# A fused packed-attention and feed-forward kernel: a new order of steps for the start, batch 0 in 256 and 320 tokens, batch 1's first shares turned by TensorE, and one remainder's products ahead of the packs

## The chip, the cores and the metric

One core of a Trainium2 chip runs the whole program. The metric is the device time of one execution in microseconds; a figure for a kernel is the median of several runs. The engines are TensorE (PE: products, and transposes with an identity), VectorE (DVE), ScalarE (ACT), GpSimd (POOL) and SyncE (SP), whose queue issues nearly all transfers. Each works off its own list in order and waits on semaphores for the others.

## The reference

```
p_packed = softmax(p k^T / 8) v             8 batches, 8 heads, 576 tokens, 32 packs, 64 dimensions
out      = softmax(q p_packed^T / 8) p_packed
x        = out, heads side by side          (4608 tokens, 512)
h        = x w_in                           (512 x 2048)
y        = (h * sigmoid(h)) w_out           (2048 x 512)
```

All in float32; the weights `w_in` and `w_out` come to the device as the bits of float64 numbers, and the kernel makes float32 numbers of them itself.

## The kernel before, in words

`p_packed` is never multiplied by the second shares. For each batch the kernel multiplies the 32 packs of each head into `w_in` (the class `Packs`: "pack products", 64-row tiles, line 232 through `heads`), which gives a small matrix per batch; the hidden layer is then the second shares times that matrix. Products of full size are taken in three terms of a rounded upper part (`hi`) and the remainder (`lo`): the upper part is rounded by ScalarE (`upper`, `g_values`), the lower is a subtraction on VectorE (`lower`, line 225, 464, 493, 551).

The work is cut into units of one batch and 128 of the 2048 hidden columns. A unit has `h` (`h_products`, line 525: 12 products, 288 tokens wide), `g` (`h_values`, lines 543 to 546: the activation of `h` on ScalarE), `l` (`h_lower`, line 551) and `o` (`out_products`, line 561: 12 products, 512 wide). The first four units of batch 0 (`u < WHOLE`) are taken in plain float32, each in two halves of the tokens (`h0.0` and `h0.1`). Of each half's 288 tokens 256 go through `o` in the unit; the 32 left over are kept in `rest`, for two batches together, and make four "rest" units, each of 12 products. `out_rows` (lines 588 to 612) takes the sums out of PSUM.

Per batch the attention goes through steps that the code names by a letter: `aS1.0` is `scores2` of batch 1, half 0. First attention: `as` scores, `ac` copy, `am` maximum, `ax` exponential (line 278), `at` turning of the shares (`turned1`, lines 285 to 297), `ay` (`spread1`, lines 299 to 316), `aa` packed products (line 330), `an` normalising (340), `ai` and `aj` the turned packs (349, 353). Second attention: `aS` scores, `aT` blockwise transposes on VectorE, `aM` maximum and subtraction (`less2`), `aX` exponential, `aD` sum, reciprocal and multiplication (`shares2`), `aH` and `aL` upper and lower part. Batch 0 alone holds its scores by tokens (`ON_TOKENS`): `aC` copies them (374), `aB` turns them on TensorE (382), and `aU` turns the shares back (402, 404), `aF` copies them out (449).

For batch 0, `turned1` transposes on TensorE. For the others VectorE transposes blocks of 32 (line 291) and `spread1` moves the blocks with 16 transfers issued by SP (line 309).

The weights come in 20 chunks, the first eight of 512 columns a partition, the others of 1024. `FIRST` and `CHUNKS` take `w_in` and `w_out` in turn. A chunk passes `wf` (fetch, line 186), `ws` (two operations of ScalarE, 192 and 193), `wz` (bound and sign, 197 and 198, on VectorE), `wj` (shift on VectorE, 204, and addition, 205: VectorE for `w_in`, POOL for `w_out`), and for `w_out` `wu` and `wl` (221, 225). `PLACES` says where the raw bits wait: in one of two staging buffers, or in the part of `win` that is filled later; a fetch into a place that is still in use waits on SP, with all that stands behind it in SP's list.

The order of all this up to the 32nd unit is written in the string `ORDER`, whose steps are put into the engines' lists as they stand. `W6` is six products with the identity that keep TensorE busy (line 139). PSUM has two double buffers for sums (`sum_banks`, two pairs) and two for everything else (`two_banks`: pack products, scores, hidden products). After `ORDER` a loop runs over the remaining units, the four rest units of batches 0 and 1 first, where `packs_in(2, 1, 2)` makes two pack products for batch 2.

Of the kernel before, what the change touches and what calls it, by code (L numbers as in the profile page):

```python
# [11 lines left out]
I32 = mybir.dt.int32  # L12
# [22 lines left out]
REST = HS - MAIN  # L35

# [17 lines left out]
W6 k0 as0.0 W1 as0.1 am0.0 wf0 wf1 am0.1 ax0.0 ax0.1 ar0 v0 ws0 wz0 W4 at0.0 ay0.0 at0.1 ay0.1 wf2 ws1 ws2 wj0 W7  # L54
aa0 an0 W1 ai0 wz2 aj0 q0 W1 pp0 aS0.0 aC0.0 pu0 W1 aS0.1 aB0.0 aC0.1 wj2 pp1 wz1 wj1 wf3 ws3 aM0.0 aX0.0 wf4 ws4
aB0.1 aM0.1 aX0.1 aD0.0 W15 aU0.0 wf5 ws5 wf6 ws6 aD0.1 wz4 aF0.0 W2 h0.0 pu1 k1 g0.0 wz6 aU0.1 aF0.1 wj6 as1.0
ac1.0 wu1 h1.0 g1.0 wf7 wf8 aH0.1 wz5 h0.1 g0.1 h1.1 ws7 v1 wz3 as1.1 wj3 ac1.1 wj5 wj4 g1.1 am1 o0.0 ax1.0 ax1.1
pp3 wz7 wj7 wf9 pp2 pu2 o1.0 at1.0 at1.1 pu3 o0.1 h2.0 h2.1 ws8 g2.0 g2.1 ws9 aL0.1 wz8 o1.1 h3.0 h3.1 wf10 ws10 wj8
# [5 lines left out]
l14 h15 ws16 o13 g15 l15 ax2.0 h16 wz16 wl15 ax2.1 h17 o14 o15 wf17 wj16 g16 l16 wf18 h18 g17 e15.1 l17 e15.0 h19
ws17 o16 wz17 wj17 g18 l18 ws18 o17 pp8 wf19 o18 at2.0 at2.1 ay2 g19 l19 pu8 ws19 pl8 h20 g20 h21 o19 wz18 h22 wj18
wu18 ar2 l20 wz19 wj19 g21 h23 wl18 o20 l21 o21 wu19 wl19 g22 l22 aa2 g23 l23 an2 pp9 pu9 pl9 pp10 o22 pu10 pl10 h24
h25 o23 b0 e23.0 g24 h26 l24 e23.1 o24 g25 ai2 l25 o25 g26 l26 aj2 aS2.1 aT2.1 aM2.1 aX2.1 aS2.0 aT2.0 o26 h27 h28
g27 l27 aM2.0 g28 l28 h29 o27 aD2.1 g29 aX2.0 h30 aH2.1 h31 l29 aD2.0 o28 o29 g30 l30 g31 l31 aH2.0 aL2.0 aL2.1 o30
o31 g32 b1 l32 v3 e31.0 pp11 pu11 e31.1 pl11 k3
# [4 lines left out]

ON_TOKENS = (0,)
# [8 lines left out]
def packed_attention_ffn(ctx: ExitStack, tc: tile.TileContext, pkT, qT, v, w_in, w_out, out):  # L84
# [26 lines left out]
    ident = const.tile([P, P + 352], F32, name="ident")  # L111
# [55 lines left out]
    class Weights:  # L167
# [22 lines left out]
        def scale(self, n):  # L190
            low, up = self.raw[n]
            nc.scalar.activation(low, low.bitcast(U32), AF.Copy, scale=2.0**-29)  # L192
            nc.scalar.activation(up.bitcast(F32), up.bitcast(F32), AF.Copy, scale=2.0**-112)  # L193

        def sign(self, n):
            low, up = self.raw[n]
            nc.vector.tensor_scalar(up.bitcast(F32), up.bitcast(F32), TOP, -TOP, op0=ALU.min, op1=ALU.max)  # L197
            nc.vector.scalar_tensor_tensor(low, up, -(2**31), low, op0=ALU.bitwise_and, op1=ALU.bitwise_or)  # L198

        def join(self, n):  # L200
            f, nf, inner = CHUNKS[n]
            low, up = self.raw[n]
            z = win[:, f : f + nf].rearrange("p f i n -> p (f i n)") if inner else self.whole(n).bitcast(I32)
            nc.vector.tensor_scalar(z, up, 3, None, op0=ALU.logical_shift_left)  # L204
            (nc.vector if inner else nc.gpsimd).tensor_tensor(z, z, low, ALU.add)  # L205
# [20 lines left out]

    def heads(bank, lhs, rhs):

        for par in range(2):
            r = slice(D * par, D * par + D)  # L230
            for i in range(NI):
                nc.tensor.matmul(bank(par)[NP * i : NP * i + NP], lhs(r, i), rhs(r, i), start=True, stop=True)  # L232
# [4 lines left out]
    class Attention:  # L237
# [3 lines left out]
        def __init__(self, b):  # L241
            self.b, self.half, self.turns, self.back, self.shares = b, {}, {}, {}, {}
# [42 lines left out]
        def turned1(self, par):  # L285
            if self.b:

                if par == 0:
                    self.turn = scratch(S)
                blocks = self.turn.rearrange("p (t r x) -> p t r x", r=2, x=NP)  # L290
                nc.vector.transpose(blocks[:, :, par], self.e1[:, par].rearrange("p (t x) -> p t x", x=NP))
                return
            ps = self.turns[par] = sum_banks()
            for c in range(5):
                n = min(P, S - c * P)
                bank = ps[:n, 1, :P] if c == 4 else ps[:n, 0, c * P : c * P + P]
                nc.tensor.transpose(bank, self.e1[:, par, c * P : c * P + n], ident)

        def spread1(self, par=None):
            if not par:  # L300
                self.e1T = scratch(5 * P)
            if self.b:

                self.e1T = self.e1T.rearrange("p (c i rx) -> p c i rx", c=5, i=NI)
                for i in range(NI):
                    for at in range(P // NP):
                        some = self.turn[NP * i : NP * i + NP].rearrange("p (t rx) -> p t rx", rx=2 * NP)
                        some = some[:, at :: P // NP]
                        nc.sync.dma_start(self.e1T[NP * at : NP * at + NP, : some.shape[1], i], some)
# [59 lines left out]
        def copied2(self, hf):  # L369
# [3 lines left out]
            at = slice(0, HS + REST) if hf == 0 else slice(HS + REST, S)  # L373
            nc.scalar.copy(self.s2[:, :, at], self.half[hf][:, :, : at.stop - at.start])

        def spread2(self, hf):
# [3 lines left out]
            for par in range(2):  # L380
                for c, s in enumerate((HS + REST, HS + REST + P) if hf else (0, P, HS + REST - P)):
                    nc.tensor.transpose(ps[:, par, P * c : P * c + P], self.s2[:, par, s : s + P], ident)
# [12 lines left out]
        def back2(self, hf):  # L395

            ps = self.back[hf] = two_banks() if self.b else sum_banks()
            left = slice(P - REST * (2 - hf), P - REST * (1 - hf))
            for par in range(2):
# [3 lines left out]
                some = self.half[0][1][left, par, MAIN:]  # L403
                nc.tensor.transpose(ps[:, par, MAIN:HS], some, ident[left, left])

        def less2(self, hf):
            if self.b in ON_TOKENS:
# [4 lines left out]
                nc.vector.tensor_tensor(t, ps, each, ALU.subtract)  # L412
# [5 lines left out]
            nc.vector.tensor_tensor(s2v, s2v, each, ALU.subtract)  # L418
# [9 lines left out]
        def shares2(self, hf):  # L428
            if self.b in ON_TOKENS:
# [5 lines left out]
                nc.vector.tensor_tensor(t, t, each, ALU.mult)  # L435
                return
            s2, e2 = self.half[hf]
# [6 lines left out]
            nc.vector.tensor_tensor(e2v, e2v, each, ALU.mult)  # L444
            nc.vector.transpose(s2, e2)

        def whole2(self, hf):
            a2 = made["whole", hf] = self.shares[hf] = a2p.tile([P, 2, HS], F32, name="a2_lo")
            nc.scalar.copy(a2, self.back[hf][:, :, :HS])

        def upper2(self, hf):
            hi = a2p.tile([P, 2, HS], F32R, name="a2_hi")
            lo = a2p.tile([P, 2, HS], F32R, name="a2_lo")
# [57 lines left out]
    def h_products(u, hf=None):  # L511
# [4 lines left out]
        for h in range(2)[half_or_all(hf)]:  # L516
# [6 lines left out]
            for n, (p, a, par) in enumerate(todo):  # L523
                bank = ps[:, h if hf is None else 0, :HS]
                nc.tensor.matmul(bank, p[:, par, cols], a[:, par], start=(n == 0), stop=(n == len(todo) - 1))  # L525

    def h_values(u, hf=None):
# [12 lines left out]
        ps, to = made.pop(("h", u, hf)), rest[:, f, b % 2]  # L540
# [5 lines left out]
        nc.scalar.activation(to, ps[..., MAIN:HS], AF.Silu)  # L546
# [41 lines left out]
    def out_rows(u, h):  # L588
# [3 lines left out]
        if more:  # L592
            o = osb.tile([P, 2, DM], F32, name="o")
            half = DM // 2
            nc.scalar.copy(o[:, 0, :half], sums[:, 0, :half])
            nc.vector.tensor_copy(o[:, 0, half:], sums[:, 0, half:])
# [17 lines left out]
    def load_parts(b):  # L614
# [18 lines left out]
        "wz": weights.sign,  # L633
# [11 lines left out]
    names |= dict(n="scaled1", i="turned", j="packs", S="scores2", T="turned2", M="less2", X="exps2", D="shares2")  # L645
# [101 lines left out]
def _laid_out(q, k, v, p, moe_w_in, moe_w_out):  # L747
# [40 lines left out]
```

## Time and profile before

| | us |
|---|---|
| median of 3 runs (lowest, highest) | 710.49 (709.82, 710.53) |
| the profiled execution | 710.59 |
| its span | 708.8 |
| TensorE busy | 696.7 |
| VectorE busy | 332.4 |
| ScalarE busy | 328.5 |
| POOL busy | 21.0 |

The span runs from the first to the last instruction that the profiler recorded; the execution's own time is 1.8 us more. A busy TensorE means that some product was under way; since products overlap and their ends are modelled, their durations add up to more than that. In the rows of instructions the first number is the start, the second the duration, then come engine, line, operation, what is written and read, its shape, the count where several were merged, and in brackets the idle time before it with what ended that. In the rows of stretches the columns are the stretch, its length, the busy time of PE, PEld (weight load), DVE, ACT and POOL, the clock granted to TensorE as a share of full speed, the share of the DMA engines, and GB/s.

### The profile page before, as it was taken

To read this page: it belongs to the slowest core of one execution; us is meant where nothing else is said; L and a number is where in the kernel's file an instruction comes from. 1 tells how busy PE (TensorE), PEld (TensorE's weight loads), DVE (VectorE), ACT (ScalarE), POOL (GpSimd) and SP (SyncE) were. 2 spreads that over 40 slices of the span, in tenths; PEclk is the share of its full clock that TensorE was granted. 3 is DMA by queue.
4 is the path that set the end of the run, shared out by engine and by line. 5 is a ranking of instruction groups with operands and counts; after the bars stand their busy time and mean duration, and the time that the engine had idled before them with its cause. 6 is when DMAs were issued, how large, how long until landed. Compare 5 with 4: busy or idle time off the path is not lost.

```text
span 708.8 us, 12103 instructions
## 1 busy us (share of the span) xinstructions
PE 696.7 (98%) x5060; PEld 564.7 (80%) x5060; DVE 332.4 (47%) x491; ACT 328.5 (46%) x614; POOL 21.0 (3%) x16
## 2 busy tenths in 40 slices
PE   8999999999999999999999999999999999999997
PEld 6647779877868888888888888878878788888886
DVE  4989985944642346332552315433362333622112
ACT  4896858634534325362542625453353533533221
POOL 0202020100000000000000000000000000000000
PEclk9999999999999999999999999999999999999999
DMA  9755653315032140302212022121301210010002
GB/s 356 304 205 198 222 218 149 125 60 193 0 130 82 34 147 1 127 21 84 75 60 83 18 88 75 41 87 36 144 1 64 79 35 2 1 59 1 1 1 74
DMA packets 30869, 65.20 MB, mean 92 GB/s; under 512 B 19296, under 2 KB 19296, under 8 KB 26464
## 3 DMA queue, kind: packets, MB, share of 16 engines
q1 hardware_dynamic: 30720, 64.30, 25.1%
q8 instruction: 40, 0.66, 0.4%
q10 hardware_dynamic: 96, 0.13, 0.1%
q14 instruction: 13, 0.11, 0.0%
HBM read 48.76 MB, written 11.53 MB: 85 GB/s over the span
## 4 chain that ended last, share of the span: by engine, by line
PE 91%; DVE 5%; ACT 2%; issue 1%; DMA 1%; DVEq 0%; ACTq 0%
PE ps_acc L561 55%; PE ps_two L525 27%; PE ps_two L232 6%; PE ps_two L330 1%; DVE win L198 1%; DMA kvq_t<-in_pkT 1%; PE ps_acc L232 0%; ACT tm L278 0%; DVE win L204 0%; ACT w_raw L192 0%; ACT w_raw L193 0%; DVE w_raw L198 0%; ACT L543 0%; DVE win L197 0%; DVE win L205 0%
## 5 line engine op out<-in xcount | busy, mean ns | idle before, releaser
L561 PE MATMUL ps_acc<-wo_hi,g_hi 128*128 128x512 f32 x560 | 222.5, 397 | 0.0
L561 PE MATMUL ps_acc<-wo_lo,g_hi 128*128 128x512 f32 x560 | 219.0, 391 | 0.0
L561 PE MATMUL ps_acc<-wo_hi,g_lo 128*128 128x512 f32 x560 | 219.0, 391 | 0.1
L551 DVE TENSOR_TENSOR g_lo<-g,g_hi 128x512 fp32r<-128x512 f32 x124 | 89.2, 720 | 256.5 <-ACT g_hi L545 256.4
L543 ACT ACTIVATE g<-ps_two 128x512 f32<-128x512 f32 x124 | 74.4, 600 | 265.4 <-PE ps_two L525 236.4
L525 PE MATMUL ps_two<-a_lo,pw_hi 128*128 128x288 f32 x528 | 156.2, 305 | 0.2
L525 PE MATMUL ps_two<-a_hi,pw_hi 128*128 128x288 f32 x496 | 147.1, 297 | 1.0 <-ACT rest L546 1.0
L525 PE MATMUL ps_two<-a_hi,pw_lo 128*128 128x288 f32 x496 | 145.9, 294 | 0.0
L561 PEld LDWEIGHTS ps_acc<-wo_hi,g_hi 128*128 128x128 f32 x560 | 105.1, 188 | 38.7 <-issue 19.4
L561 PEld LDWEIGHTS ps_acc<-wo_hi,g_lo 128*128 128x128 f32 x560 | 105.1, 188 | 23.7 <-DVE g_lo L551 0.8
L561 PEld LDWEIGHTS ps_acc<-wo_lo,g_hi 128*128 128x128 f32 x560 | 105.2, 188 | 18.0
L525 PEld LDWEIGHTS ps_two<-a_lo,pw_hi 128*128 128x128 f32 x528 | 99.2, 188 | 6.8 <-ACT rest L546 0.9
L525 PEld LDWEIGHTS ps_two<-a_hi,pw_hi 128*128 128x128 f32 x496 | 93.3, 188 | 5.6 <-ACT rest L546 1.3
L525 PEld LDWEIGHTS ps_two<-a_hi,pw_lo 128*128 128x128 f32 x496 | 93.2, 188 | 0.0
L545 ACT ACTIVATE g_hi<-ps_two 128x512 fp32r<-128x512 f32 x124 | 73.6, 593 | 7.8 <-PE ps_acc L561 7.8
L493 DVE TENSOR_TENSOR pw_lo<-ps_two,pw_hi 128x1024 fp32r<-128x1024 f32 x31 | 36.8, 1219 | 9.5 <-ACT pw_hi L490 9.5
L490 ACT CAST pw_hi<-ps_two 128x1024 fp32r<-128x1024 f32 x31 | 30.2, 1019 | 16.0 <-PE ps_two L232 16.0
L232 PE MATMUL ps_two<-win,ppT 64*32 64x512 f32 (+1 forms) x560 | 32.7, 559 | 2.6 <-DVE pw_lo L493 1.6
L546 ACT ACTIVATE rest<-ps_two 128x64 f32<-128x64 f32 (+1 forms) x132 | 30.4, 230 | 0.0
L232 PEld LDWEIGHTS ps_two<-win,ppT 64*32 64x32 f32 x560 | 8.2, 105 | 17.8 <-issue 10.3
L543 ACT ACT_TABLE_LOAD x16 | 20.5, 1283 | 2.0 <-PE ps_two L525 1.9
L535 ACT CAST g_hi<-rest 128x512 fp32r<-128x512 f32 x16 | 9.9, 623 | 14.1 <-PE ps_acc L561 13.7
(116 smaller groups left out, 479.4 us busy)
## 6 DMA issues: line engine op xcount, KB each, us to landing
kvq_t<-in_v SPq DMA_DIRECT2D x8, 1280.0 KB, 6.4
kvq_t<-in_pkT SPq DMA_DIRECT2D x7, 1216.0 KB, 6.9
out<-o SPq DMA_DIRECT2D x16, 512.0 KB, 2.8
kvq_t<-in_qT SPq DMA_DIRECT2D x7, 1152.0 KB, 5.2
w_raw<-in_w_in SPq DMA_DIRECT2D x6, 1024.0 KB, 6.4
win<-in_w_out SPq DMA_DIRECT2D x3, 1024.0 KB, 5.7
w_raw<-in_w_out SPq DMA_DIRECT2D x3, 1024.0 KB, 4.8
tm<-tm SPq DMA_DIRECT2D x56, 40.0 KB, 1.9
```

Of the source, the lines that this page charges most:

```text
L198: nc.vector.scalar_tensor_tensor(low, up, -(2**31), low, op0=ALU.bitwise_and, op1=ALU.bitwise_or)
L232: nc.tensor.matmul(bank(par)[NP * i : NP * i + NP], lhs(r, i), rhs(r, i), start=True, stop=True)
L330: nc.tensor.matmul(self.ps[NP * i : NP * i + NP, par * D : par * D + D], e, vs[:n, c, h * D : h * D + D], start=(c == 0), stop=(c == 4),)
L490: nc.scalar.copy(self.hi, self.ps[:, :, : self.nf * P])
L493: nc.vector.tensor_tensor(self.lo, self.ps[:, :, : self.nf * P], self.hi.bitcast(F32), ALU.subtract)
L525: nc.tensor.matmul(bank, p[:, par, cols], a[:, par], start=(n == 0), stop=(n == len(todo) - 1))
L535: nc.scalar.copy(g_hi, g)
L543: nc.scalar.activation(g, ps[..., :MAIN], AF.Silu)
L545: nc.scalar.activation(g_hi, ps[..., :MAIN], AF.Silu)
L546: nc.scalar.activation(to, ps[..., MAIN:HS], AF.Silu)
L551: nc.vector.tensor_tensor(g_lo[:, c], g[:, c], g_hi[:, c].bitcast(F32), ALU.subtract)
L561: nc.tensor.matmul(bank, g[:, rows], w[:, at], start=(first and n == 0), stop=(last and n + 1 == len(todo)))
```

## The change

Five things change.

- Batch 0's tokens, held by tokens, are cut into a first half of 256 (`MAIN`) and a second of 320 (`MORE`), instead of 320 and 256 in the scores and 288 and 288 in the shares and the hidden products. The remainder of 64 tokens lies all in the second half. Batches 1 to 7 stay at 288.
- `turned1` and `spread1` of batch 1 go the way of batch 0: ten transposes on TensorE into `two_banks`, copied out by ScalarE, instead of two transposes on VectorE and 16 transfers.
- Steps become smaller. Of a weight chunk, `ws` now scales the upper word, `wr` rounds the lower, `wz` bounds, `wg` joins the sign, `wt` shifts and `wj` adds. Of the second attention, `aM` is the maximum, `aE` the subtraction, `aD` the sum and reciprocal, `aG` the multiplication.
- `ORDER` is written anew with them, and the additions run on POOL for the 13 chunks in `ON_POOL` instead of the 10 chunks of `w_out`.
- In the loop, the first rest unit's output products stand ahead of batch 2's two pack products, not behind them. The rest rows are copied from PSUM by ScalarE alone (512 columns) instead of 256 by ScalarE and 256 by VectorE.

```diff
+MORE = MAIN + 2 * REST
...
 ORDER = """
+W7 k0 as0.0 W1 as0.1 am0.0 ax0.0 am0.1 wf0 v0 W4 at0.0 ay0.0 ax0.1 wf1 ws0 at0.1 ay0.1 wr0 wz0 wg0 ar0 W3 aa0 an0 W1
+ai0 ws1 q0 wr1 wf2 aj0 wt0 W1 aS0.0 aC0.0 wz1 wt1 ws2 wj0 wg1 W2 aB0.0 aM0.0 aE0.0 aX0.0 wr2 wf3 wz2 wt2 aS0.1 aC0.1
+wf4 wf5 W11 aB0.1 ws3 wr4 k1 wf6 ws4 aD0.0 pp0 pu0 wg2 wj2 aG0.0 aU0.0 pp1 wr5 aM0.1 aF0.0 W1 h0.0 aE0.1 pu1 aX0.1
+wz4 g0.0 wf7 h1.0 g1.0 wj1 wz3 wr3 aD0.1 aG0.1 ws6 W2 as1.0 wg3 wf8 ac1.0 as1.1 aU0.1 ac1.1 aF0.1 o0.0 wr6 ws5 wr7
+h0.1 g0.1 ws8 h1.1 wt4 wt3 wj3 wg4 wj4 pp2 pu2 wz6 wz5 o0.1 g1.1 wt6 wg5 wt5 wr8 h2.0 ws7 wf9 ws9 g2.0 h2.1 g2.1 am1
+ax1.0 ax1.1 wz8 wj5 wf10 wg6 wj6 wr9 o1.0 o2.0 wg8 at1.0 pp3 ay1.0 pu3 wt8 wj8 o1.1 ws10 wz7 wr10 wt7 wg7 at1.1 wz9
+wt9 ay1.1 wg9 h3.0 g3.0 v1 wj7 o2.1 wj9 wz10 wu1 ar1 wf11 h3.1 g3.1 aH0.0 wg10 wt10 wj10 aL0.0 pp4 pu4 pl4 ws11 aa1
+o3.0 an1 ai1 aH0.1 wr11 aj1 q1 aL0.1 h4 o3.1 wf12 wz11 aS1.0 wg11 wt11 k2 wj11 wu10 wl10 aT1.0 aM1.0 g4 l4 wu3 wl3
+aE1.0 wu11 h5 g5 aS1.1 aX1.0 l5 wu7 o4 h7 aT1.1 aM1.1 aE1.1 aD1.0 wu5 wf13 aX1.1 aD1.1 h6 g6 wl11 ws12 l6 o5 o6
...
+g14 o13 pp7 l14 wr14 wz16 wg14 g15 wt14 o14 pu7 l15 pl7 wj15 wu15 wl15 wj14 wu14 wl14 wf17 h16 g16 h17 ar2 l16 wg16
...
+wj19 h23 h22 o20 v2 l21 g23 o21 l23 wu19 wl19 g22 l22 aa2 an2 pp10 pu10 ai2 o22 pl10 aj2 aS2.0 aT2.0 b0 aS2.1 aT2.1
+aM2.1 o23 e23.1 e23.0 aM2.0 h24 h25 g24 h26 l24 o24 g25 h27 l25 k3 o25 aE2.0 aX2.0 aD2.0 g26 l26 g27 aG2.0 aH2.0 h28
+aE2.1 h29 o26 l27 aX2.1 g28 l28 o27 aD2.1 h30 g29 l29 h31 o28 g30 o29 aG2.1 aH2.1 aL2.1 l30 o30 g31 l31 o31 g32
+aL2.0 l32 b1 e31.0 e31.1 pp11 pu11 v3 pl11
...
+ON_POOL = (0, 1, 2, 6, 9, 10, 11, 13, 14, 15, 16, 18, 19)
...
-    ident = const.tile([P, P + 352], F32, name="ident")
+    ident = const.tile([P, P + 16], F32, name="ident")
...
         def join(self, n):
-            f, nf, inner = CHUNKS[n]
-            low, up = self.raw[n]
-            z = win[:, f : f + nf].rearrange("p f i n -> p (f i n)") if inner else self.whole(n).bitcast(I32)
-            nc.vector.tensor_scalar(z, up, 3, None, op0=ALU.logical_shift_left)
-            (nc.vector if inner else nc.gpsimd).tensor_tensor(z, z, low, ALU.add)
+            z, low = self.float32(n), self.raw[n][0]
+            (nc.gpsimd if n in ON_POOL else nc.vector).tensor_tensor(z, z, low, ALU.add)
...
+    def tokens_in(b, hf):
+        return HS if b else MORE if hf else MAIN
...
         def turned1(self, par):
-            if self.b:
+            if self.b >= EARLY:
...
-            ps = self.turns[par] = sum_banks()
+            ps = self.turns[par] = two_banks() if self.b else sum_banks()
...
-            copy = nc.scalar.copy if par else nc.vector.tensor_copy
+            copy = nc.scalar.copy if par or self.b else nc.vector.tensor_copy
...
             o = osb.tile([P, 2, DM], F32, name="o")
-            half = DM // 2
-            nc.scalar.copy(o[:, 0, :half], sums[:, 0, :half])
-            nc.vector.tensor_copy(o[:, 0, half:], sums[:, 0, half:])
+            nc.scalar.copy(o[:, 0], sums[:, 0])
...
         if more:
+            hidden_up_to(u + 1 if u == n_early else u + 2)
+            out_products(u)
             if u == n_early:
                 packs_in(2, 1, 2)
-            else:
-                hidden_up_to(u + 2)
-            out_products(u)
```

More of the change, by code (lines that the diff above doesn't have):

```diff
@@ L53 @@
 ORDER = """
[L54 to L58, printed above, removed]
@@ L64 @@
[L64 to L68, printed above, removed]
@@ L241, in __init__ @@
         def __init__(self, b):
-            self.b, self.half, self.turns, self.back, self.shares = b, {}, {}, {}, {}
+            self.b, self.half, self.turns, self.back, self.shares, self.most = b, {}, {}, {}, {}, {}
         def scores1(self, hf):
@@ L380, in spread2 @@
             for par in range(2):
-                for c, s in enumerate((HS + REST, HS + REST + P) if hf else (0, P, HS + REST - P)):
+                for c, s in enumerate((MAIN, MAIN + P, S - P) if hf else (0, P)):
                     nc.tensor.transpose(ps[:, par, P * c : P * c + P], self.s2[:, par, s : s + P], ident)
@@ L397, in back2 @@
             ps = self.back[hf] = two_banks() if self.b else sum_banks()
-            left = slice(P - REST * (2 - hf), P - REST * (1 - hf))
+            left = slice(P - 2 * REST, P)
             for par in range(2):
@@ L402, in back2, with largest2 @@
                     nc.tensor.transpose(ps[:, par, at], self.half[hf][1][:, par, at], ident)
-                some = self.half[0][1][left, par, MAIN:]
-                nc.tensor.transpose(ps[:, par, MAIN:HS], some, ident[left, left])
-        def less2(self, hf):
+                if hf:
+                    some = self.half[hf][1][left, par, MAIN:]
+                    nc.tensor.transpose(ps[:, par, MAIN:MORE], some, ident[left, left])
+        def largest2(self, hf):
             if self.b in ON_TOKENS:
@@ L411, in less2 @@
                 nc.vector.tensor_reduce(mx, ps, axis=AX.X, op=ALU.max)
-                nc.vector.tensor_tensor(t, ps, each, ALU.subtract)
+                self.most[hf] = t, ps, each
                 return
@@ L417, in less2, with minus2 @@
             each = mx2.rearrange("p (g o) -> p g o", o=1).broadcast_to([P, 2 * NB, NP])
-            nc.vector.tensor_tensor(s2v, s2v, each, ALU.subtract)
+            self.most[hf] = s2v, s2v, each
+        def minus2(self, hf):
+            t, s, each = self.most[hf]
+            nc.vector.tensor_tensor(t, s, each, ALU.subtract)
+        def less2(self, hf):
+            self.largest2(hf)
+            self.minus2(hf)
         def exps2(self, hf):
@@ L434, in shares2 @@
                 nc.vector.reciprocal(sm, sm)
-                nc.vector.tensor_tensor(t, t, each, ALU.mult)
+                self.most[hf] = t, each
                 return
-            s2, e2 = self.half[hf]
+            _, e2 = self.half[hf]
             e2v = e2.rearrange("p (g x) -> p g x", x=NP)
@@ L443, in shares2, with times2 @@
             each = sm.rearrange("p (g o) -> p g o", o=1).broadcast_to([P, 2 * NB, NP])
-            nc.vector.tensor_tensor(e2v, e2v, each, ALU.mult)
-            nc.vector.transpose(s2, e2)
+            self.most[hf] = e2v, each
+        def times2(self, hf):
+            e, each = self.most[hf]
+            nc.vector.tensor_tensor(e, e, each, ALU.mult)
+            if self.b not in ON_TOKENS:
+                nc.vector.transpose(*self.half[hf])
+        def shares2(self, hf):
+            self.sums2(hf)
+            self.times2(hf)
         def whole2(self, hf):
-            a2 = made["whole", hf] = self.shares[hf] = a2p.tile([P, 2, HS], F32, name="a2_lo")
-            nc.scalar.copy(a2, self.back[hf][:, :, :HS])
+            n = tokens_in(0, hf)
+            a2 = made["whole", hf] = self.shares[hf] = a2p.tile([P, 2, MORE], F32, name="a2_lo")[:, :, :n]
+            nc.scalar.copy(a2, self.back[hf][:, :, :n])
         def upper2(self, hf):
-            hi = a2p.tile([P, 2, HS], F32R, name="a2_hi")
-            lo = a2p.tile([P, 2, HS], F32R, name="a2_lo")
+            n = tokens_in(self.b, hf)
+            hi = a2p.tile([P, 2, MORE], F32R, name="a2_hi")[:, :, :n]
+            lo = a2p.tile([P, 2, MORE], F32R, name="a2_lo")[:, :, :n]
             made["a2", self.b, hf] = hi, lo
@@ L539, in h_values @@
         g, g_hi = (x.rearrange("p (h s) -> p h s", h=2) for x in hidden[u][:2])
-        ps, to = made.pop(("h", u, hf)), rest[:, f, b % 2]
+        banks = ps = made.pop(("h", u, hf))
+        to = rest[:, f, b % 2]
         if hf is not None:
@@ L545, in h_values @@
             nc.scalar.activation(g_hi, ps[..., :MAIN], AF.Silu)
-        nc.scalar.activation(to, ps[..., MAIN:HS], AF.Silu)
+        if b:
+            nc.scalar.activation(to, ps[..., MAIN:HS], AF.Silu)
+        elif hf != 0:
+            nc.scalar.activation(rest[:, f, 0].rearrange("p h s -> p (h s)"), banks[:, 1 if hf is None else 0, MAIN:MORE], AF.Silu)
     def h_lower(u, hf=None):
@@ L632, in packed_attention_ffn @@
         "ws": weights.scale,
-        "wz": weights.sign,
+        "wr": weights.round,
+        "wz": weights.bound,
+        "wg": weights.sign,
+        "wt": weights.shift,
         "wj": weights.join,
@@ L644, in packed_attention_ffn @@
     names = dict(s="scores1", c="copied1", m="largest1", x="exps1", r="shares1", t="turned1", y="spread1", a="packed")
-    names |= dict(n="scaled1", i="turned", j="packs", S="scores2", T="turned2", M="less2", X="exps2", D="shares2")
+    names |= dict(n="scaled1", i="turned", j="packs", S="scores2", T="turned2", M="largest2", E="minus2")
+    names |= dict(X="exps2", D="sums2", G="times2")
     names |= dict(F="whole2", H="upper2", L="lower2", U="back2", C="copied2", B="spread2")
@@ L759, in _laid_out @@
         half = qT[b].reshape(P, 2, NI, HS)
-        tokens_of_b = np.concatenate([half[:, 0], np.roll(half[:, 1], REST, axis=2)], axis=2)
-        at = [tokens_of_b[:, :, : HS + REST], tokens_of_b[:, :, HS + REST :]]
+        second = [half[:, 1, :, :MAIN], half[:, 0, :, MAIN:], half[:, 1, :, MAIN:]]
+        at = half[:, 0, :, :MAIN], np.concatenate(second, axis=2)
         qT[b] = np.concatenate([x.reshape(P, -1) for x in at], axis=1)
```

42 lines of the change are left out of this document (25 added, 17 removed).

## The prediction

> **What bounds the kernel now.** I read the page first, then the chain of work that ended last, then the first 65 us in order of time, engine by engine.
>
> ```profile
> span 708.8 us, 12103 instructions
> ...
> PE 91%; DVE 5%; ACT 2%; issue 1%; DMA 1%; DVEq 0%; ACTq 0%
> ```
>
> TensorE holds 91% of the chain, and the change leaves the number of its products alone. What can move is the other 9%: where the chain is not on TensorE. The chain in order of time says where that is (start, us, what):
>
> ```profile
> 62.12 1.55 DVE g_lo L551
> ...
> 63.72 2.56 PE ps_acc L561 x10
> 66.28 3.19 PE ps_two L525 x24
> ...
> 84.78 2.77 PE ps_acc L561 x12
> ...
> 173.01 1.28 ACT L543
> ...
> 704.57 0.38 ACT o L595
> ...
> 704.98 0.42 DVE o L596
> ```
>
> Up to 63.7 us the chain lies mostly on VectorE; from there to the last product it is TensorE but for two holes (at 173 and at 196 us), and a tail behind 704.5. So three places pay: the start, the two holes, the tail. In between, TensorE has no idle time to win, only to lose. The 24 products of 288 columns in 3.19 us give 133 ns each.
>
> **The clock in the start.** The same trace by stretches (TensorE busy in the third column, the granted clock in the eighth):
>
> ```profile
> 13.00:14.00 1.00, 0.41 (x29) 0.44 (x32) 0.97 (x4) 1.00 (x3) 0.00 (x0) 1.00 1.01 421
> ...
> 24.00:25.00 1.00, 0.00 (x0) 0.00 (x0) 0.96 (x3) 1.00 (x3) 0.00 (x0) 1.00 1.09 436
> ...
> 27.00:31.00 4.00, 3.92 (x26) 2.26 (x26) 3.86 (x8) 2.31 (x5) 0.00 (x0) 0.57 0.79 333
> ```
>
> TensorE stands idle for the whole stretch 24 to 25, and from 27 to 31 it is granted 0.57: (1 - 0.57) x 4 = 1.7 us of work lost. The smaller hole at 13 had no such sequel.
>
> **The change, part by part: the start.** The rows from which the new start is added up, in order of time:
>
> ```profile
> 9.63 1.61 PE L297 MATMUL ps_acc<-ident,tm 128*128 128x128 f32 x10
> ...
> 11.45 0.57 ACT L315 COPY tm<-ps_acc 128x512 f32<-128x512 f32 x1
> ...
> 12.04 0.69 DVE L198 SCALAR_TENSOR_TENSOR w_raw<-w_raw 128x512 int32<-128x512 int32 x1
> ...
> 12.65 0.68 DVE L315 COPY tm<-ps_acc 128x512 f32<-128x512 f32 x1
> ...
> 13.59 1.73 PE L330 MATMUL ps_acc<-kvq_t,tm 128*32 128x64 f32 x80 [0.79 <-DVE tm L316]
> ...
> 16.10 0.27 ACT L353 COPY ppT<-ps_acc 128x128 f32<-128x128 f32 x1 [1.54 <-PE ps_acc L349]
> ...
> 17.57 0.70 ACT L374 COPY tm<-ps_acc 128x640 f32<-128x640 f32 x1 [1.20 <-PE ps_acc L232]
> ...
> 18.36 0.87 PE L382 MATMUL ps_acc<-ident,tm 128*128 128x128 f32 x6
> 18.53 0.59 ACT L374 COPY tm<-ps_acc 128x512 f32<-128x512 f32 x1
> 18.80 0.42 DVE L204 TENSOR_SCALAR o<-w_raw 128x512 int32<-128x512 int32 x1
> ...
> 19.27 0.96 DVE L411 TENSOR_REDUCE on_tokens<-ps_acc 128x24 f32<-128x768 f32 x1
> ...
> 19.83 0.66 PE L382 MATMUL ps_acc<-ident,tm 128*128 128x128 f32 x4
> ...
> 21.13 0.68 DVE L411 TENSOR_REDUCE on_tokens<-ps_acc 128x16 f32<-128x512 f32 x1
> ...
> 23.19 0.61 ACT L423 ACTIVATE tm<-tm 128x512 f32<-128x512 f32 x1
> ...
> 25.85 0.25 DVE L434 RECIPROCAL on_tokens<-on_tokens 128x16 f32<-128x16 f32 x1
> ...
> 27.07 2.04 PE L525 MATMUL ps_two<-a_lo,pw_hi 128*128 128x288 f32 x4
> ...
> 32.57 1.42 POOL L205 TENSOR_TENSOR o<-o,w_raw 128x512 int32<-128x512 int32 x1 [11.97 <-DVE o L204]
> 32.74 1.53 DVE L204 TENSOR_SCALAR win<-win 128x512 int32<-128x512 int32 x1
> ```
>
> Step 1. The packing products (`aa0`, L330) start at 13.59 because VectorE's copy L315 comes behind two operations on weight chunk 0 (bound, then the sign at 12.04). In the new list `ay0.0` stands ahead of them, and its input, the first half of the ten transposes from 9.63, is there by 10.5. Then ScalarE's copy (11.45 + 0.57, and its small one) is last, and the products start at 12.15: 1.4 us earlier. The normalised packs come behind chunk 0's bound, sign and the reciprocals on VectorE, which end about when the products do (13.9), so the copy at 16.10 becomes one at 14.7.
>
> Step 2. First half of 256 tokens instead of 320: its scores start at 15.0 (the four products on `win` that stood ahead now come later) and end at 15.7; copy 0.59 instead of 0.70, to 16.3; four transposes instead of six, 0.66 instead of 0.87, to 17.0. VectorE has by then done shift, bound, shift and sign of chunks 0 and 1 and is held once by POOL's new add for chunk 0. The last two rows price such a hold: POOL works to 33.99, and a VectorE operation of about 0.4 us takes 1.53, so 1.1 us. That makes VectorE free at 17.35, 0.3 us after the transposes. Maximum at 17.35 against 19.27.
>
> Step 3. Maximum 0.68, subtraction the same, exponential 0.61: 19.4, with two small weight operations beside the exponential, 19.5. Sum, epsilon and reciprocal (0.68 + 0.2 + 0.25, with gaps 1.2): 20.7. Then the sign of chunk 2 (0.69) stands ahead of the multiplication, a loss, and the multiplication ends at 22.1. Four transposes to 22.8, the copy on ScalarE behind its list of weight pieces to 23.6 or 24.1. First hidden product `h0.0`: 23.9 against 27.07, 3.2 us earlier.
>
> Step 4. Batch 1's first shares turned on TensorE: ten transposes as in the row at 9.63 add 1.6 us to TensorE, all of it on the path. What they replace, and the rest of the feed:
>
> ```profile
> 40.48 1.44 DVE L291 STREAM_TRANSPOSE tm<-tm 128x576 f32<-128x576 f32 x2 [1.63 <-ACT tm L278]
> ...
> 42.01 10.41 SPq L309 DMA_DIRECT2D tm<-tm  x16
> ...
> 51.18 0.69 DVE L197 TENSOR_SCALAR win<-win 128x1024 f32<-128x1024 f32 x1
> ...
> 51.41 1.09 PE L232 MATMUL ps_two<-win,ppT 64*32 64x512 f32 x16 [0.87 <-DVE win L205]
> ...
> 51.98 1.23 DVE L198 SCALAR_TENSOR_TENSOR win<-win 128x1024 int32<-128x1024 int32 x1
> ...
> 54.02 2.33 POOL L205 TENSOR_TENSOR win<-win 128x1024 int32<-128x1024 int32 x1 [13.80 <-DVE win L204]
> ...
> 62.92 0.50 PE L561 MATMUL ps_acc<-wo_hi,g_hi 128*128 128x512 f32 x1
> ```
>
> 1.44 us of VectorE and 10.4 us of SP's queue go; four copies go to ScalarE (11.45's 0.57 and a small one, twice, 1.6 us), which delays `g3.0` but nothing that TensorE waits for: `o2.1` lies between.
>
> Step 5. Does the earlier start last? Follow VectorE from 22.1 to chunk 9, whose pack products wait at 51.41 today: second half's maximum and subtraction (2 x 0.96), its sum to multiplication (2.5), 13 operations on chunks 3 to 6 (6.6), batch 1's maximum (1.5), 13 on chunks 5 to 9 by 0.4, 0.69 or 1.23 each (10.1), and holds by POOL (1.5): 46.2. There POOL takes chunk 9, and its 2.33 ends at 48.5. TensorE itself, adding its list from 23.9 without waits, is there at 47.4, or at 49.1 if the slow clock stays. So VectorE and POOL, not the clock, set this point: 48.5 against 51.41, 2.9 us earlier, with Step 4's 1.6 inside. From there the next late arrival is batch 1's normalised packs (VectorE: chunk 10's bound held by POOL, then 2.3 us more of weights, the lower parts of shares and packs, 53.9); TensorE has only 4.6 us of work until then and waits about 0.8. Then come two hidden units, half an output step and two scores, 6.5 us, and the output products of unit 4 at 60.4 instead of 62.92: **-2.5 us**, the term of the start. Its ends: nothing won where VectorE falls behind by that much (0), and Step 3 undisturbed (-4.2).
>
> Half widths of 256 and 320 in batch 0's 12 later units keep the sum of columns: 72 products at 256 and 72 at 320 for 144 at 133 ns. No row shows 256 columns of this type. If weight loading kept the narrow ones at 133, it would be 72 x 15 ns = 1.0 us; if time goes with columns, 0. The 512-column products (12 in 2.77 us, 231 ns) show it going with columns nearly, so 0.
>
> Splitting the weight steps adds no instruction: 20 chunks still have two ScalarE, three VectorE and one addition each, now 13 additions on POOL instead of 10. Three chunks of 512 come back to VectorE, six go. I charge the holds above and nothing after 63 us, where TensorE is ahead by output products.
>
> **The holes and the tail.** Rows of TensorE and of the tail, with the idle time in brackets:
>
> ```profile
> 175.56 0.40 PE L525 MATMUL ps_two<-a_hi,pw_hi 128*128 128x288 f32 x1 [1.03 <-ACT rest L546]
> ...
> 197.73 1.09 PE L232 MATMUL ps_two<-win,ppT 64*32 64x512 f32 x16 [1.57 <-DVE pw_lo L493]
> ```
>
> The first: ScalarE waited for batch 2's exponential, loaded a function table each way (1.28) and released the buffer for `h28` late. The new list has these scores five output steps earlier and the two exponentials apart, each with two output steps (2.7 us each) behind it: -1.0. The second: three pack products in a row with two buffers. The remainder's twelve products, 2.7 us, now stand between, and cover the 1.57: **-1.6**. Next late there is nothing: the buffer is free at 197.7, and the third product now stands at 199. The tail: two copies that ran one after the other (704.57 to 705.40) become one of 512 columns, 0.6 as at 11.45: -0.2.
>
> Sum: -2.5 - 1.0 - 1.6 - 0.2 = -5.3. The profiled execution took 710.6 us (span 708.8), 0.1 above the median of 710.5: **705.2 us**.
>
> **The rivals.** (a) *The start is not kept.* VectorE is the chain to 63.7, and its work hardly shrinks; if the holds by POOL eat what Step 1 to 3 win, only holes and tail are left: 710.5 - 2.8 = 707.7; with Step 4's 1.6 uncovered 709.3. For it: the holds; against: 1.44 us less VectorE work, and a first half that needs less of it.
>
> (b) *The clock stays low after the start, and matters.* New idle pieces between 21.7 and 23.9 are at most 0.5 us, nearest to the stretch at 13, after which the clock stayed; but much of that time is transposes. If the feed is better than Step 5, the 1.7 us show: 706.5. The Trainium skill (TensorE: Matmul & The Clock Gate, Part 4: PE-mode transpose) says that transposes do not count as busy for the clock as products do; by that rule the low clock would come back and this rival hold. The trace leaves it open: its dip follows idle time and transposes together.
>
> (c) *A new wait in the middle.* From 63.7 to 172 us the trace has none, the order of all of it is new, and one more hole like the two shown costs 1.0 to 1.6: 706.5.
>
> (d) *Slower.* SP issues in order; a transfer of this size lands 6.4 us after its issue:
>
> ```profile
> kvq_t<-in_v SPq DMA_DIRECT2D x8, 1280.0 KB, 6.4
> ```
>
> Chunks 9, 10 and 11 now stand ahead of batch 1's values and queries, and chunk 11 needs chunk 7's place, which I have free at 46.3. Values and queries then land about 7 us later, for use at 49 and 57. From about 50.5 on each microsecond that chunk 7 is late is one on the path; at 58 the result is over 712. For it: one engine's list decides it; against: 4 us of slack, and 16 issues gone.
>
> (e) *The change does nothing*: the start as in (a) with 1.6 uncovered, and one new hole: 710.4.
>
> **How the numbers follow.** Forecast 705.2, 0.45 (own range 703.7 to 706.2); better still (Step 3 undisturbed) 703.2, 0.07; (a) 0.18; (b) 0.07; (c) 0.08; (e) 0.08; (d) 0.07. The range goes from 702.9 to 709.3: it leaves out (d), (e) and a little below. A change under 0.2% (1.4 us) can't be told from none here. Faster 0.84, same 0.08, slower 0.08.
>
> **What would show it.** `h0.0` near 24 (Steps 1 to 3), pack products of chunk 9 near 48.5, unit 4's output near 60.4; no wait of a microsecond at the third pack product of batch 2; one copy ahead of the last store; granted clock in the stretch 24 to 31. I am wrong if TensorE waits between 63 and 170 us, or if `h0.0` is early and 60.4 isn't.

## The result and the profile after

| | before | after |
|---|---|---|
| median, us (lowest, highest) | 710.51 (709.82, 710.59) | 704.34 (703.09, 704.99) |
| ratio, 95% interval | | 0.9913 [0.9901, 0.9925] |
| profiled execution, its span | 710.59, 708.8 | 703.09, 701.3 |
| first hidden product `h0.0` | 27.07 | 23.22 |
| pack products of chunk 9 | 51.41 | 47.45 |
| output products of unit 4 | 62.92 | 58.53 |

The kernel is 0.87% faster; the forecast was 705.2, 0.75%. The profiled execution of the changed kernel is its fastest, so its own difference, 7.5 us, is larger than that of the medians, 6.2. Two later sets of runs gave medians of 703.6 and 704.4 on other occasions, and profiled executions of 703.5 and 703.7, each again the fastest of its set. A few executions took far longer than all others of their kernel (853.67 us in one of these sets); medians, ratios and profiles in this text are without them.

The page of the changed kernel, span and chain:

```profile
span 701.3 us, 12059 instructions
...
PE 97%; ACT 1%; DMA 1%; DVE 1%; issue 0%; ACTq 0%; DVEq 0%
```

TensorE's share of the chain goes from 91% to 97%. The chain in order of time shows how early it turns to TensorE for good (start, us, what):

```profile
22.26 0.47 ACT a_lo L486
22.76 0.38 ACT pw_hi L528
23.22 1.98 PE ps_two L563 x8
25.20 0.38 ACT g_hi L582
25.62 0.73 PE ps_two L144 x4
26.39 1.20 PE ps_two L250 x32
27.59 0.37 PE ps_acc L420 x2
```

Before, VectorE led until 63.7 us. Now TensorE leads from 23.2 on, but for 0.4 us at 25.2, where it waits for a buffer. Ahead of 23.2 the chain lies on ScalarE without a break from 17.94 on: weight pieces and copies, of which the first two lines are the last. The same three stretches as before (columns as there), and the whole middle as one row:

```profile
13.00:14.00 1.00, 0.93 (x13) 0.66 (x5) 0.90 (x4) 0.34 (x2) 0.05 (x1) 1.00 1.00 406
24.00:25.00 1.00, 1.00 (x6) 0.70 (x4) 0.96 (x2) 1.00 (x1) 0.00 (x0) 1.00 1.07 434
27.00:31.00 4.00, 4.00 (x36) 1.98 (x21) 3.45 (x8) 3.42 (x7) 0.00 (x0) 1.00 0.41 129
...
60.00:188.00 128.00, 128.00 (x883) 105.91 (x882) 88.59 (x118) 79.70 (x131) 13.59 (x6) 1.00 0.37 125
```

TensorE is no longer idle at 24, its clock stays at 1.00 from 27 to 31, and from 60 to 188 us it is busy throughout: the wait at 175 is gone and no new one has come. The pack products of batch 2 and the tail:

```profile
188.41 1.09 PE L250 MATMUL ps_two<-win,ppT 64*32 64x512 f32 x16
192.39 1.95 PE L250 MATMUL ps_two<-win,ppT 64*32 64x512 f32 x32
...
697.34 0.59 ACT L636 COPY o<-ps_acc 128x512 f32<-128x512 f32 x1 [7.81 <-PE ps_acc L603]
```

The remainder's products now lie between the first pack products and the other two, which follow each other without a wait; one copy of 0.59 us stands ahead of the last transfers, and 4.0 us pass from the last product to the end of the span instead of 4.3.

### The profile page after: what moved, and what is told of

It is laid out like the page before. It is cut to its first block, busy times and chain, and to the rows that moved or that the text cites. A ratio compares the mean times of both kernels' runs of the same rounds, so it can differ in the third digit from the quotient of the medians.

```text
span 701.3 us, 12059 instructions
## 1 busy us (share of the span) xinstructions
PE 693.3 (99%) x5058; PEld 560.5 (80%) x5058; DVE 326.2 (47%) x482; ACT 331.0 (47%) x614; POOL 28.7 (4%) x19
## 4 chain that ended last, share of the span: by engine, by line
PE 97%; ACT 1%; DMA 1%; DVE 1%; issue 0%; ACTq 0%; DVEq 0%
PE ps_acc L603 58%; PE ps_two L563 29%; PE ps_two L250 7%; PE ps_two L348 2%; DMA kvq_t<-in_pkT 1%; PE ps_acc L250 0%; ACT tm L296 0%; PE ps_two L144 0%; ACT tm L392 0%; ACT w_raw L201 0%; ACT win L201 0%; PE ps_two L315 0%; PE ps_two L367 0%; PE ps_acc L315 0%; DVE mx L286 0%
## 5 line engine op out<-in xcount | busy, mean ns | idle before, releaser
L563 PE MATMUL ps_two<-a_lo,pw_hi 128*128 128x288 f32 (+2 forms) x528 | 154.6, 301 | 0.1
L563 PE MATMUL ps_two<-a_hi,pw_hi 128*128 128x288 f32 (+1 forms) x496 | 146.5, 295 | 0.0
L563 PE MATMUL ps_two<-a_hi,pw_lo 128*128 128x288 f32 (+1 forms) x496 | 145.9, 294 | 0.0
L586 ACT ACTIVATE rest<-ps_two 128x64 f32<-128x64 f32 x112 | 25.9, 231 | 0.0
L573 ACT CAST g_hi<-rest 128x512 fp32r<-128x512 f32 x16 | 9.9, 624 | 13.5 <-PE ps_acc L603 13.2
```

The lines of the kernel that those rows point to most:

```text
L573: nc.scalar.copy(g_hi, g)
```

## The experiments

All kernels were timed beside the kernel before. The places are those of their profiles, in us.

| kernel | median | ratio to before, 95% | `h0.0` | packs, chunk 9 | unit 4's outputs |
|---|---|---|---|---|---|
| changed kernel again | 703.63 | 0.9903 [0.989, 0.9917] | 23.20 | 47.42 | 58.51 |
| packs first | 705.40 | 0.9929 [0.9916, 0.9941] | 23.56 | 47.79 | 58.88 |
| old POOL list | 704.56 | 0.9915 [0.9902, 0.9929] | 23.59 | 48.26 | 59.35 |
| old turning | 720.62 | 1.0138 [1.012, 1.0156] | 23.34 | 50.68 | 76.03 |
| split alone | 710.77 | 1.0002 [0.9993, 1.0012] | 26.93 | 51.93 | 63.38 |
| split undone, again | 706.36 | 0.9953 [0.9937, 0.9969] | 24.93 | 50.15 | 61.52 |
| fewer warm products | 704.54 | 0.9923 [0.991, 0.9936] | 24.04 | 48.18 | 59.26 |
| turning alone, again | 713.67 | 1.0043 [1.0021, 1.0066] | 26.37 | 54.83 | 66.11 |
| two warm steps out | 703.98 | 0.9912 [0.9899, 0.9926] | 22.58 | 46.67 | 57.76 |
| changed kernel, third | 704.37 | 0.9919 [0.9905, 0.9932] | 23.37 | 47.59 | 58.68 |

**The changed kernel again.**

> The changed kernel once more. Theory A (the start, the two holes and the tail give what the first profile shows, 4.4 + 2.8 + 0.3 us): median 703 to 705, first hidden product near 23.2, unit 4's output products near 58.5 in this profile too, and the 1.9 us between the four runs so far is the phase of TensorE's clock window at the start. Rival B (the first profile was a lucky execution): unit 4's output products at 59.5 to 60.5 in this profile, where the sum of the prediction had them, and a median of 704.5 to 705.5.

Theory A's places hold to 0.02 us (23.20, 58.51), in the third profile to 0.15. The packs-first kernel has the same start and gives 23.56 and 58.88. So in the profiles the start is worth 4.0 to 4.4 us. In the medians it may be less: they differ by 6.2 us in the first set, which leaves 3.0 for the start if everything behind it is worth the 3.2 that the first profile shows. That the spread of its runs comes from TensorE's clock was not shown, and the runs speak against it: every one from 703.09 to 705.27 has a mean granted clock of 0.999 or 1.000. The three profiles differ by 0.4 us at one place, the packed products of batch 2 at 144 us (1.77 us in the first, 2.20 and 2.11 in the others), and nothing in them accounts for runs up to 705.3.

**Packs first.**

```diff
         if more:
-            hidden_up_to(u + 1 if u == n_early else u + 2)
-            out_products(u)
             if u == n_early:
                 packs_in(2, 1, 2)
+            else:
+                hidden_up_to(u + 2)
+            out_products(u)
```

> The changed kernel with batch 2's two pack products ahead of the first remainder's output products again. Theory A (the three pack products in a row on two buffers make the hole): TensorE waits 1.5 to 1.7 us for the lower part at the third of them again, 1.6 us longer than the changed kernel. Rival B (in the new order the buffer is free early enough): under 0.5 us longer, no such wait.

TensorE's rows of this kernel at that place:

```profile
189.39 1.95 PE L250 MATMUL ps_two<-win,ppT 64*32 64x512 f32 x32
...
192.91 1.09 PE L250 MATMUL ps_two<-win,ppT 64*32 64x512 f32 x16 [1.57 <-DVE pw_lo L531]
```

Theory A holds. The wait of 1.57 us is back to the hundredth, and the median is 1.8 us above the changed kernel's on the same chip. The profiled executions are 2.0 us apart: the 1.57, and a start that was 0.4 later in this one. This term of the sum stands.

**Old POOL list.**

```diff
-ON_POOL = (0, 1, 2, 6, 9, 10, 11, 13, 14, 15, 16, 18, 19)
+ON_POOL = (1, 3, 5, 7, 10, 11, 14, 15, 18, 19)
```

> The changed kernel with the additions on POOL for the chunks of w_out alone, as before: six additions go back to VectorE, three to POOL. Theory A (from the first hidden product on TensorE has stock, so holds and additions on VectorE are hidden): within 0.5 us of the changed kernel. Rival B (holds by POOL set the start, as Step 5 of the prediction had it): 0.5 to 1.5 us faster, with the pack products of chunk 9 ahead of 47. Rival C (POOL relieves VectorE ahead of the first hidden product): first hidden product 0.5 us later or more and the time with it.

Rival B falls: without the added POOL work the pack products of chunk 9 come later, not earlier. The transposes that turn the first half's shares back wait 0.8 us for VectorE instead of at most 0.3. How much that costs depends on the profile beside it: against the changed kernel's first, `h0.0` is 0.4 later and unit 4's outputs 0.8; against packs first, which has the changed kernel's start, 0.03 and 0.5. That goes toward rival C, at less than its 0.5 us for `h0.0`. The median is 0.2 to 0.9 above the changed kernel's, with intervals that overlap, so no difference in the total is shown.

**Old turning in the new order.** In `turned1`, `spread1` and `packed` the condition `self.b >= EARLY` is `self.b` again; the 16 transfers stand where `ay1.1` does.

```diff
-            if self.b >= EARLY:
+            if self.b:
```

> The changed kernel with batch 1's first shares turned by VectorE and 16 transfers again, at the places where the new order has these steps. Theory A (TensorE is the bound there and its ten transposes cost 1.1 us net): TensorE wins 1.1 us by the transposes but waits for the packed products, whose 16 transfers take 10.4 us of SP's queue from about 45 on: 5 to 8 us slower. Rival B (the transposes on TensorE are the costlier way, as the 1.6 us of Step 4 say, and transfers are hidden): 0.5 to 1.1 us faster.

Theory A in kind, far off in size: 17 us, not 5 to 8. SP's list and the packed products of this kernel:

```profile
45.44 10.42 SPq L329 DMA_DIRECT2D tm<-tm  x16
55.90 0.59 SPq L169 DMA_DIRECT2D kvq_t<-in_v  x1
```
```profile
62.02 3.37 PE L350 MATMUL ps_two<-kvq_t,tm 128*32 128x64 f32 x80 [9.38 <-issue]
```

I had priced the 16 transfers alone. Batch 1's values stand behind them on SP, go out at 55.90 and are used 6.1 us later, at 62.02, where the changed kernel has these products at 48.5. TensorE waits 9.4 us there (the profile names no releaser), after 4.1 us for POOL's addition to chunk 9. These 13.5 us are not all of the 17. Behind the waits the granted clock stays low (columns as above):

```profile
62.00:66.00 4.00, 3.98 (x81) 3.04 (x82) 0.29 (x1) 1.61 (x2) 0.00 (x0) 0.50 1.00 424
66.00:70.00 4.00, 4.00 (x10) 2.01 (x9) 3.36 (x4) 1.83 (x4) 0.26 (x1) 0.50 1.03 421
```

(1 - 0.50) x 8 = 4 us of work lost, and the pack products of chunk 9, between the two waits, take 1.96 us instead of 1.09. With the 1.1 us that TensorE saves on transposes this gives about 17.3; unit 4's outputs are 17.5 later. So this is the mechanism of the prediction's rival (d), set off by the transfers rather than by chunk 7.

**Split alone.** The old order with 256 and 320 tokens for batch 0, old additions, turning, loop and tail; each old step is written as its new parts:

```diff
-W7 k0 as0.0 W1 as0.1 am0.0 ax0.0 am0.1 wf0 v0 W4 at0.0 ay0.0 ax0.1 wf1 ws0 at0.1 ay0.1 wr0 wz0 wg0 ar0 W3 aa0 an0 W1
+W6 k0 as0.0 W1 as0.1 am0.0 wf0 wf1 am0.1 ax0.0 ax0.1 ar0 v0 wr0 ws0 wz0 wg0 W4 at0.0 ay0.0 at0.1 ay0.1 wf2 ...
...
```

> The kernel before with batch 0 in 256 and 320 tokens as the only change: the old order step by step, the old additions on POOL, the old turning of batch 1, the old loop and tail. Theory A (the narrow first half brings the first hidden product forward, but in the old order VectorE and the second half set what follows): first hidden product 1 to 2 us earlier than before (27.07), total 0 to 1 us faster. Rival B (the split carries the start): 2 to 4 us faster.

The total fits theory A, the way does not: `h0.0` comes only 0.14 us earlier, and the total is unchanged within 0.1%. TensorE's row shows where the rest goes:

```profile
26.93 1.13 PE L562 MATMUL ps_two<-a_lo,pw_hi 128*128 128x256 f32 x4 [0.65 <-ACT a_lo L485]
```

The first half is smaller, but ScalarE's copy of it stands behind weight pieces in the old list.

**Split undone in the new order.** `load_q`, `copied2`, `spread2`, `on_tokens`, `back2`, `whole2`, `h_values` and the layout are those of before. There are two sets of runs; the profile is from the second.

```diff
-        return HS if b else MORE if hf else MAIN
+        return HS
```

> The changed kernel with batch 0 in 320 and 256 tokens for the scores and 288 and 288 for shares and hidden products, as before; new order, loop, turning and tail stay. Theory A (the order and the split share the start): first hidden product 1 to 2 us later than in the changed kernel, total 1 to 2 us slower. Rival B (the order carries all of it): within 0.5 us. Rival C (the split carries most): 3 us slower or more.

> The changed kernel with batch 0's old split once more, since the profile of the first time fell on a disturbed execution. By its times (706.3 to 707.9) theory A of that run holds and more: first hidden product 2 to 3 us later than 23.2, unit 4's output products 2.5 to 4 us later than 58.5. Rival: first hidden product only 1 us later and the rest a new wait behind it, at the second half or in the remainders.

Medians 707.5 and 706.4, so 2 to 4 us above the changed kernel, more than theory A of the first set said. In the new order `h0.0` is 1.6 to 1.7 us later without the split, between the two theories of the second set, and unit 4's outputs 2.8 to 3.0 later, as its theory A says. Part of it is TensorE's clock:

```profile
24.00:27.00 3.00, 2.85 (x23) 1.92 (x24) 2.18 (x7) 2.73 (x4) 0.00 (x0) 0.64 1.02 416
27.00:31.00 4.00, 3.94 (x45) 2.52 (x44) 1.54 (x4) 2.12 (x6) 0.00 (x0) 0.84 0.09 35
```

(1 - 0.64) x 3 + (1 - 0.84) x 4 = 1.7 us of work lost. So the split is worth an earlier first half, and in this profile the clock too. How much is the clock alone was not tried apart, but the eleven runs of this kernel order themselves by their mean granted clock: 704.99 and 705.22 at 0.999, 706.00 to 707.15 at 0.997 and 0.998, 707.78 to 709.29 at 0.994 and 0.995. At 0.999 it is only 0.6 to 1.6 us above the changed kernel's medians; the rest goes with the clock. With the new order the split pays, by itself it does not.

**Fewer warm products.**

```diff
-wf4 wf5 W11 aB0.1
+wf4 wf5 W1 aB0.1
```

> The changed kernel with one product with the identity instead of eleven while TensorE waits for the second half's scores. Theory A (the clock falls after idle TensorE time, as at 27 us in the kernel before): a stretch at a granted clock of about 0.5 within 24 to 31 us and 0.5 to 1.7 us longer. Rival B (the later feed sets the start, so a low clock there is hidden): the low clock shows, the total within 0.4 us. Rival C (a hole of 2.5 us is too short): no low clock, same time.

```profile
20.00:24.00 4.00, 3.89 (x44) 2.46 (x44) 3.77 (x7) 3.36 (x8) 1.67 (x1) 0.63 0.99 406
```

The result lies between A and B. The hole before the second half's transposes is now 2.4 us, the clock falls (0.37 x 4 = 1.5 us lost), `h0.0` and unit 4's outputs are 0.8 later, and the median is 0.2 to 0.9 above the changed kernel's. So in the places the warm products earn about half of what the clock costs; in the total the intervals overlap.

**Two warm steps out.**

```diff
-aG0.0 aU0.0 pp1 wr5 aM0.1 aF0.0 W1 h0.0 aE0.1
+aG0.0 aU0.0 pp1 wr5 aM0.1 aF0.0 h0.0 aE0.1
...
-aD0.1 aG0.1 ws6 W2 as1.0
+aD0.1 aG0.1 ws6 as1.0
```

> The changed kernel without two of its steps of products with the identity: the one ahead of the first hidden product and the two behind the second hidden product (25.6 to 26.4 us, which first wait 0.4 us for a buffer). Theory A (from the first hidden product on TensorE is the bound, so whatever leaves its list there leaves the time): first hidden product 0.3 to 0.4 us earlier, unit 4's output products 0.4 to 1.1 us earlier, total 0.4 to 1.1 us below the changed kernel. Rival B (the multiplication of the second half on VectorE, which ends at 26.4, sets the next step): under 0.3 us. Rival C (the clock falls in the hole): slower by 0.2 to 1.5 us.

> The changed kernel as the measure for the three kernels beside it. Both theories: 703.5 to 704.5.

Against the third profile of the changed kernel, from the same chip, `h0.0` is 0.8 earlier, twice what theory A says, unit 4's outputs are 0.9 earlier, as it says, and the clock stays at 1.00. Yet the median of 703.98 lies among those of the changed kernel. TensorE's row at the packed products of batch 2 shows where the gain goes:

```profile
144.43 2.29 PE L348 MATMUL ps_two<-kvq_t,tm 128*32 128x64 f32 x76 [0.94 <-ACT rest L588]
```

There TensorE waits 0.94 us for ScalarE to release a buffer; in the changed kernel these products start at 144.13 to 144.33 with no wait. So the lead of 0.9 us is given back there, all of it. Why the buffer is a different one there was not tried.

**Turning alone.** The kernel before with `turned1`, `spread1` and `packed` of the changed one:

```diff
-pp3 wz7 wj7 wf9 pp2 pu2 o1.0 at1.0 at1.1 pu3 o0.1 h2.0
+pp3 wz7 wj7 wf9 pp2 pu2 o1.0 at1.0 ay1.0 at1.1 ay1.1 pu3 o0.1 h2.0
...
-o2.1 pp4 aL0.0 o3.0 ay1 aa1
+o2.1 pp4 aL0.0 o3.0 aa1
```

> The kernel before with batch 1's first shares turned by TensorE and copied by ScalarE as the only change; each half is copied out right after its transposes. Theory A (in the old order the 16 transfers were hidden: the packed products at 54.35 waited for nothing; TensorE pays 1.1 us, VectorE, which sets the old start, wins 1.4): within 0.7 us of the kernel before. Rival B (the way of turning is worth as much by itself as in the new order, where undoing it cost 17 us): 3 us faster or more. Rival C (TensorE's 1.1 us show in full): 1 to 2 us slower.

> The kernel before with batch 1's turning on TensorE alone, once more for an undisturbed profile. Its times of the first run (3 to 4 us slower) refute all three theories of that run. Theory D (the two buffers in PSUM that the transposes now take are what it costs: the copies stand on ScalarE behind exponentials and weight pieces, and TensorE waits for the buffers in order): waits of TensorE at the transposes of 1.5 to 2.5 us in total, and unit 4's output products 3 to 4 us later than 62.9. Rival C again (only the transposes' own 1.1 us): no wait at them.

The first set (median 713.7) went against all three theories; the second has the profile:

```profile
40.05 0.77 PE L297 MATMUL ps_two<-ident,tm 128*128 128x128 f32 x5 [2.26 <-ACT pw_hi L490]
...
41.70 1.08 PE L297 MATMUL ps_two<-ident,tm 128*128 128x128 f32 x5 [0.88 <-ACT tm L316]
```

Theory D holds in kind: 2.26 + 0.88 = 3.1 us of waits for PSUM buffers at the transposes (more than the 2.5 I gave), and unit 4's outputs at 66.1, 3.2 later than before. The total is 3.3 us slower. The waits are not the whole cost: behind the first of them the granted clock falls,

```profile
40.00:44.00 4.00, 3.07 (x12) 2.01 (x13) 0.00 (x0) 1.92 (x6) 0.00 (x0) 0.75 0.80 292
44.00:48.00 4.00, 4.00 (x12) 2.37 (x11) 2.00 (x3) 3.78 (x6) 0.00 (x0) 0.82 0.71 298
```

by (0.25 + 0.18) x 4 = 1.7 us of work; how the 3.3 us divide between buffers and clock was not tried apart. In the changed kernel the same transposes stand one half at a time, far apart, and wait for nothing. The profile of the split alone, in the old order too, shows a granted clock of 1.00 from 27 to 31 and no gain from it at unit 4's outputs (63.38). Yet the low clock of the kernel before was not free: of its 39 runs beside the experiments the twenty at a mean granted clock of 1.000 have a median of 709.87, the six at 0.995 and 0.996 one of 711.1. Its profiled execution is one of 0.996.

## Why the prediction was right, and where its terms were off

The time, the sign and the two later terms held; the largest term, the start, came out 1.9 us larger in the profile than forecast, and what sets it is not what the prediction named (Step 5). That the median is only 0.9 us below the forecast is luck in part: the profiles differ by 7.5 us, the medians by 6.2, and where the rest of the start's gain goes in the slower runs no profile shows.

- *Step 1* (-1.4 to the packed products): right in kind, 0.8 short. They start at 11.37, not 12.15. ScalarE's copy was last, as said, but starts at 10.80, not at 11.45. About 0.5 of that is luck: the scores of batch 0's second half took 0.72 us in this execution and 1.21 in that of before, and with packs first, where they took 0.87, the products start at 11.78.
- *Step 2*: the maximum at 16.43, not 17.35; of the 0.9, 0.7 come from Step 1. The hold by POOL is there: the shift of chunk 1 takes 1.40 us beside POOL's first addition.
- *Step 3*: the multiplication ends at 21.0, not 22.1, and `h0.0` starts at 23.2, not 23.9; part of that lead is lost to the second pack product, which waits 0.4 for POOL.
- *Step 4*: the transposes cost 2 x 0.55 us of the chain, not 1.6. I took the whole row. Its 1.61 holds its drain, which the next product overlaps on a busy TensorE (five of the transposes have 0.71 in their row at 40.31 and 0.55 in the chain), and its second five need the exponential that ends at 10.33.

```profile
40.47 0.55 PE ps_two L315 x5
...
43.31 0.55 PE ps_two L315 x5
```

- *Step 5* is the term that was mis-sized: -2.5, measured -4.4 in the first profile. It said that VectorE and POOL set the pack products of chunk 9, at 48.5, and that TensorE then waits 0.8 for batch 1's packs. My sum for VectorE was not far off (24.1 us from the second half's maximum to POOL's start; measured 20.91 to 43.70, 22.8), but it began 1.2 late, after Steps 1 to 3, so POOL takes chunk 9 at 43.7 and not at 46.2:

```profile
43.70 2.77 POOL L220 TENSOR_TENSOR win<-win,w_raw 128x1024 int32<-128x1024 int32 x1 [5.78 <-DVE w_raw L209]
```
```profile
44.14 2.89 DVE L205 TENSOR_SCALAR win<-win 128x1024 f32<-128x1024 f32 x1
```
```profile
47.45 1.09 PE L250 MATMUL ps_two<-win,ppT 64*32 64x512 f32 x16
```

POOL is done at 46.5, and TensorE comes at 47.45 and waits for nothing; "47.4 without waits", the figure I had set aside, was the one to take. That it fits to 0.05 is luck: it counted from `h0.0` at 23.9, and TensorE's list took 24.2 us from there instead of 23.5. Of the 1.9 us, 1.05 are this point and 0.8 the wait for batch 1's packs, which did not come. The hold itself is larger than I charged (2.89 us for an operation of 0.69) and costs nothing, since the packs of batch 1, at 51.95, come while TensorE still has output products. TensorE's margin is 1.0 us at the first place and 0.4 at the second (the packs are ready at 51.11, their weight load starts at 51.52), so an error of 2.5 us in VectorE's list made two waits out of none.
- *The half widths*: 0, as taken. The chain gives 12 products, six of each width, 1.59 us, as 12 of 288 columns had 1.60.
- *The holes*: -1.0 and -1.6; both waits are gone, and packs-first brings back 1.57. From unit 4's outputs to the last product's end the profile gives 638.7 us instead of 641.6, so 2.9, which holds a wait of 0.4 at 63.3 that I had not counted. *The tail*: -0.2, measured -0.3.

Of the rivals, (a) and (d) did not occur, but old turning shows (d)'s chain of waits at full length. (c) and (e) did not: TensorE is busy for the whole of 60 to 188 us. (b) did not: the clock stayed. By the Trainium skill (TensorE: Matmul & The Clock Gate, Part 4: PE-mode transpose), with transposes not counted as busy, the low clock should have come back with the transposes and short holes of 20 to 24 us; the granted 1.00 from 27 to 31, in all three profiles, gives no sign of that. It is weak evidence, since transposes are only about 1.2 of the 3.3 us that TensorE is busy from 20 to 24. The size of the holes doesn't settle it either: fewer warm products (a hole of 2.4 us), turning alone at 40 us (2.3), the kernel before (1.3) and split undone (0.8 and 1.0) show a low clock behind them, turning alone at 24 us (1.4) doesn't.

## What to carry to other kernels

Ask in which order the work ahead of the first full product stands on each engine before asking what it costs: the same smaller first half was worth nothing in the old order and 2 to 4 us in the new, much of it through the clock, and the same transposes cost 3 us in one place and 1.1 in another. Price a step that moves by all that stands behind it in its queue, not by itself: sixteen small transfers held one large one, and with the low clock behind the waits that made 17 us. And a hold on an engine that is ahead of need is free; add the engines' lists up separately and take the later of the two, since an error of 1 us in one of them decides whether there is a wait.

## What the runs showed that I had not expected

TensorE's first scores take 1.22 us in one execution and 0.72 in another of the same kernel, though the granted clock is 1.00 in both profiles:

```profile
4.79 1.22 PE L250 MATMUL ps_acc<-kvq_t 64*32 64x288 f32 x16
```
```profile
4.72 0.72 PE L250 MATMUL ps_acc<-kvq_t 64*32 64x288 f32 x16
```

The first row is from the changed kernel's first profile, the second from its second; `h0.0` starts within 0.02 us in both, since in the second ScalarE waits 1.78 us for the fetch of a weight chunk, until 17.14. Where the fetch is not last the difference comes through: with packs first the scores took 1.22 and 0.87 us, and `h0.0` is at 23.56. The granted clock of the windows does not show how fast the first products run. And a gain of 0.9 us at 58 us into the kernel can vanish 86 us later, at a PSUM buffer, with TensorE busy all the way between.
